# Program order for the GpSimd casts, spread weight loads and a wider skew in a fused retention and MLP-mixer kernel

## Chip, cores and metric

The kernel runs on one core of a Trainium2 chip. The metric is the device time of one execution in microseconds (us), as the median of several runs. Engines are called PE (TensorE matmul), PEld (its weight loads), DVE (VectorE), ACT (ScalarE), POOL (GpSimd) and SP (SyncE, which only issues transfers here).

## What is computed

Two layers, one behind the other, for 4 batches, 768 positions, 8 heads of 64 (512 channels):

```python
gamma = 1.0 - 2.0 ** (-5.0 - np.arange(H))
for t in range(S):                                   # retention, per head
    state = gamma * state + outer(k[t], v[t])
    y[t] = scale * q[t] @ state
x = y as [B, S, H * D]
xt = x.transpose(0, 2, 1)                            # token mixing
h = np.maximum(xt @ w_tok1, 0.0) @ w_tok2            # 768 -> 256 -> 768
u = x + h.transpose(0, 2, 1)
h2 = np.maximum(u @ w_ch1, 0.0) @ w_ch2              # channel mixing, 512 -> 1536 -> 512
return u + h2
```

Inputs, weights and output are float32 in DRAM; the matmuls take float16.

## The kernel before

**Tiling.** The sequence is cut into 6 chunks of 128 positions (`NC`), in two halves of 3 (`HC`). Heads go in pairs, 4 pairs per batch (`NP`, index `p`), so a pair fills 128 partitions. The retention is computed in its chunked form: within a chunk by a masked score matrix, across chunks by a running state `U`.

**Front.** `front(b, p)` (L137) does retention and token mixing of one batch and head pair and is a generator of 11 steps (`NS`), each ended by a `yield`:
- step 0: DVE scales k to float16 (L156, two instructions), POOL casts q (L158);
- step 1: PE transposes k (L167), ACT copies it out (L169), POOL casts v (L172);
- step 2: PE transposes q;
- step 3: PE forms k'v per chunk (L189 in batch 0, L192 later), DVE chains them into `U` (L197, L199), ACT and DVE write its float16 form (L201, L202);
- steps 4, 5: scores of either half (L211), masked by DVE into `am` (L214);
- steps 6, 7: output y of either half (L224, L226), scaled into `x` by ACT (L232) or, in the second half of batches 1 to 3, by DVE with the table `gyw` (L236), then cast to float16 by POOL (L237, one cast per half);
- step 8: first token matmul (L243, 12 matmuls over both halves of `x16`), ReLU on ACT (L245);
- step 9: second token matmul (L253), DVE adds it to `x` (L256), POOL casts the sum to `u16` (L257), once per half;
- step 10: PE transposes `u16` (L263), ACT copies it into `uT` (L265, L267).

**Back.** `back(b)` does channel mixing of a batch: for each half of the sequence 12 groups of 4 matmuls over `uT` and `wc1` (L288, ReLU in L291), then 3 output tiles of 12 matmuls over `wc2` (L296), a DVE add (L301) and a store from SP (L303). It needs `uT` of all four pairs.

**Order.** `fronts(b, skew)` interleaves the four generators of a batch: step `s` of pair `p` stands at `skew * p + s`, and steps at one place go by `s`. Front 0 runs alone with skew 4. After it, a list of planned times merges the steps of back `b` with those of front `b + 1`; the back's 47 planned us (`PERIOD`) hold 44 steps of the next front, which begin 10 planned us in for batch 1 and 9 before the back for later ones, and lie evenly on 28 planned us for batch 1. This is the order in which the program is written. A scheduler then simulates the machine with its own durations and may issue instructions of an engine in another order, by readiness and place; the order that it finds is fixed in each engine's queue, and every queue is worked off in order.

**Order edges.** `keep_in_program_order` (`pin`) ties an instruction behind the one that stands last before it on the same engine in the written program; it adds no wait. Before, the k, q and v casts (L156, L158, L172) are pinned; the casts L237 and L257 and the table's eight multiplications (L317) are not. `issue_after` ties the weight loads behind the v cast of pair 1 (`wt1`, `wt2`) and of pair 3 (all three `wc1`, all three `wc2`): L106 to L114, on POOL's queue, casting from float32 on the way.

**Loads.** `load(b, p)` (L126) issues k, q and v of a pair from SP, 128 x 768 float32 (0.39 MB) each. Those of batch 1 wait until the last of the three `wc1` loads has landed.

Of the kernel before, what the change touches and what calls it, by code (L numbers as in the profile page):

```python
# [13 lines left out]
ALU = mybir.AluOpType  # L14
# [3 lines left out]
def kernel(  # L18
# [11 lines left out]
    nc = tc.nc  # L30
    B, H, S, D = q.shape
    P = 128
# [22 lines left out]
    def bank():  # L55
        return ps.tile([P, 512], FP, name="acc")
# [16 lines left out]
    gy = const_p.tile([P, H], FP, name="gy")  # L73
# [6 lines left out]
    for p in range(NP):  # L80
# [5 lines left out]
        out=mask, in_=mask, compare_op=ALU.is_ge, fill=0.0,  # L86
        base=0, pattern=[[0, HC], [1, P]], channel_multiplier=-1,
    )
    gyw = const_p.tile([P, H, D], FP, name="gyw")
# [6 lines left out]
    wt1 = const_p.tile([P, NC, DT], F16, name="wt1")  # L96
    wt2 = const_p.tile([P, NJ, S], F16, name="wt2")
    NW = 3
    FW = NF // NW
    wc1 = [const_p.tile([P, NP, FW * P], F16, name=f"wc1_{i}") for i in range(NW)]  # L100
    wc2 = [const_p.tile([P, FW, C], F16, name=f"wc2_{i}") for i in range(NW)]

    def load_weights(stage):
        first = []
        if stage == 0:
            nc.gpsimd.dma_start(out=wt1, in_=moe_w_tok1.rearrange("(i p) j -> p i j", p=P))  # L106
            nc.gpsimd.dma_start(out=wt2, in_=moe_w_tok2.rearrange("(i p) j -> p i j", p=P))
        elif stage == 1:
            for i in range(NW):
                first.append(nc.gpsimd.dma_start(  # L110
                    out=wc1[i], in_=moe_w_ch1[:, i * FW * P:(i + 1) * FW * P].rearrange(
                        "(i p) j -> p i j", p=P)))
            for i in range(NW):
                nc.gpsimd.dma_start(  # L114
                    out=wc2[i], in_=moe_w_ch2[i * FW * P:(i + 1) * FW * P].rearrange(
                        "(i p) j -> p i j", p=P))
        return first


    loaded = {}  # L120
# [1 line left out]
    def load(b, p, after=None):  # L122
        got = []
        for nm, src in (("k", k), ("q", q), ("v", v)):
            t = load_p.tile([P, 2 * NC, D], FP, name=f"{nm}f")
            dma = nc.sync.dma_start(  # L126
                out=t, in_=src[b, 2 * p:2 * p + 2].rearrange("h (c p) d -> p (h c) d", p=P))
            if after is not None:
                tc.add_manual_dep(
                    dma.ins, after.ins.name,  # L130
                    mybir.DependencyInfo(mybir.DependencyClass.Sync, mybir.DependencyReason.DATA),
                    reason="the weights come first")
            got.append(t)
        loaded[b, p] = got
# [3 lines left out]
    def front(b, p):  # L138
# [3 lines left out]
        x, uT = xs[b]  # L142
        pc = slice(p * P, (p + 1) * P)
        kf, qf, vf = loaded.pop((b, p))
        first = b == 0
        pin = tc.keep_in_program_order

        def half(hf):
            return slice(hf * HC, (hf + 1) * HC)
# [4 lines left out]
        for j in range(2):  # L154
            h = 2 * p + j
# [61 lines left out]
        x16 = att_p.tile([P, NC, P], F16, name="x16", bufs=2)  # L217
        for hf in range(2):
            y = bank()
            for i in range(HC):  # L220
                c = hf * HC + i
                o = y[:, i * P:(i + 1) * P]
                if c > 0:
                    nc.tensor.matmul(o, qT[:, c * P:(c + 1) * P], R[:, c - 1], start=True, stop=False)  # L224
                for j in range(2):
                    nc.tensor.matmul(o[:, j * D:(j + 1) * D], ams[2 * hf + j][:, i], v16[:, c, j],  # L226
                                     start=(c == 0), stop=(c == 0 or j == 1))
            yv = y[:, :HC * P].rearrange("p (i d) -> p i d", d=P)
            if hf == 0 or first:
                for j in range(2):  # L230
                    h = 2 * p + j
                    nc.scalar.mul(x[:, half(hf), h * D:(h + 1) * D], yv[:, :, j * D:(j + 1) * D],  # L232
                                  gy[:, h:h + 1])
            else:
                g = gyw[:, 2 * p:2 * p + 2].rearrange("p (o h) d -> p o (h d)", o=1)
                nc.vector.tensor_tensor(x[:, half(hf), pc], yv, g.to_broadcast([P, HC, P]), ALU.mult)  # L236
            nc.gpsimd.tensor_copy(x16[:, half(hf)], x[:, half(hf), pc])  # L237
            yield
        h1 = att_p.tile([P, NJ, P], F16, name="h1", bufs=2)
        acc = bank()  # L240
# [6 lines left out]
        u16 = att_p.tile([P, NC, P], F16, name="u16", bufs=2)  # L247
        for hf in range(2):
            acc = bank()
            for i in range(HC):  # L250
                t = slice((hf * HC + i) * P, (hf * HC + i + 1) * P)
                for jt in range(NJ):
                    nc.tensor.matmul(acc[:, i * P:(i + 1) * P], wt2[:, jt, t], h1[:, jt],  # L253
                                     start=(jt == 0), stop=(jt == NJ - 1))
            xo = x[:, half(hf), pc]
            nc.vector.tensor_tensor(xo, xo, acc[:, :HC * P].rearrange("p (i d) -> p i d", d=P), ALU.add)  # L256
            nc.gpsimd.tensor_copy(u16[:, half(hf)], xo)  # L257
        yield
        tp = ps_tp.tile([P, 1024], F16, name="tp")
        for hf in range(2):  # L260
# [11 lines left out]
    def fronts(b, skew):  # L272
        gens = [front(b, p) for p in range(NP)]
        for _, s, p in sorted((skew * p + s, s, p) for p in range(NP) for s in range(NS)):
            yield s, p, next(gens[p])
# [3 lines left out]
    def back(b):  # L279

        x, uT = xs.pop(b)
        for sh in range(2):
            h2 = mlp_p.tile([P, NF, SH], F16, name="h2")
            for ft in range(NF):
                acc = bank()
                w = wc1[ft // FW]
                for ct in range(NP):
                    nc.tensor.matmul(acc[:, :SH], w[:, ct, (ft % FW) * P:(ft % FW + 1) * P],  # L288
                                     uT[:, ct, sh * SH:(sh + 1) * SH],
                                     start=(ct == 0), stop=(ct == NP - 1))  # L290
                nc.scalar.activation(h2[:, ft], acc[:, :SH], AF.Relu)  # L291
                yield
            for i in range(HC):
                acc = bank()
                for ft in range(NF):
                    nc.tensor.matmul(acc, h2[:, ft, i * P:(i + 1) * P], wc2[ft // FW][:, ft % FW],  # L296
                                     start=(ft == 0), stop=(ft == NF - 1))
                    if ft % 4 == 3 and ft < NF - 1:
                        yield
                o = o_p.tile([P, C], FP, name="o")  # L300
                nc.vector.tensor_tensor(o, x[:, sh * HC + i], acc, ALU.add)  # L301
                t0 = (sh * HC + i) * P
                nc.sync.dma_start(out=out[b, t0:t0 + P, :], in_=o)  # L303
                yield


    for p in range(NP):
        load(0, p)
    ch1 = None
    for s, p, ins in fronts(0, 4):  # L310
        if s == 1 and p in (1, 3):
            with tc.issue_after(ins.ins):
                ch1 = load_weights(p // 3)
    for p in range(NP):
        load(1, p, after=ch1[-1])
    for h in range(H):
        nc.gpsimd.tensor_scalar(gyw[:, h], gyw[:, h], gy[:, h:h + 1], None, ALU.mult)  # L317


    FRONT_US, BACK_US, LEAD = 16.0, 31.0, 9.0  # L320
# [3 lines left out]
    def add(steps, times, kind):  # L324
        for n, t in enumerate(times):
            todo.append((t, len(todo), steps, kind))

    for b in range(B):
        t0 = b * PERIOD
        gen = back(b)  # L330
        us = BACK_STEPS
        span = PERIOD if b + 1 < B else BACK_US
        run = 0.0
        times = []
        for d in us:
            times.append(t0 + run / BACK_US * span)
            run += d
        add(gen, times, ("back", b))
        if b + 1 < B:
            f0 = t0 + 10.0 if b == 0 else t0 - LEAD  # L340
            f1 = t0 + PERIOD - LEAD
            n = NP * NS
            add(fronts(b + 1, 5), [f0 + (f1 - f0) * i / n for i in range(n)], ("front", b + 1))
    for t, _, gen, (kind, b) in sorted(todo, key=lambda e: e[:2]):
        got = next(gen)
        if kind == "front" and b + 1 < B and got[0] == 3:
# [31 lines left out]
```

## Time and profile before

| | us |
|---|---|
| median of 3 runs (247.86 to 248.69) | 248.13 |
| the profiled execution | 248.53 |
| its span, first to last instruction | 246.8 |
| PE busy | 204.7 |
| DVE busy | 120.4 |
| ACT busy | 105.8 |
| POOL busy | 69.3 |

The profiled execution lies 0.40 us above the median, and 1.7 us of it lie outside the span. All positions below are us from the span's start. In a timeline the columns are start, duration, engine, line, operation, output <- inputs, shapes and count, and in brackets the idle time of that engine just before, with what ended it.

### The profile page before, as it was taken

To read this page: it belongs to the slowest core of one execution; us is meant where nothing else is said; L and a number is where in the kernel's file an instruction comes from. 1 tells how busy PE (TensorE), PEld (TensorE's weight loads), DVE (VectorE), ACT (ScalarE), POOL (GpSimd) and SP (SyncE) were. 2 spreads that over 40 slices of the span, in tenths; PEclk is the share of its full clock that TensorE was granted. 3 is DMA by queue.
4 is the path that set the end of the run, shared out by engine and by line. 5 is a ranking of instruction groups with operands and counts; after the bars stand their busy time and mean duration, and the time that the engine had idled before them with its cause. 6 is when DMAs were issued, how large, how long until landed. Compare 5 with 4: busy or idle time off the path is not lost.

```text
span 246.8 us, 4741 instructions
## 1 busy us (share of the span) xinstructions
PE 204.7 (83%) x1908; PEld 129.2 (52%) x1908; DVE 120.4 (49%) x287; ACT 105.8 (43%) x219; POOL 69.3 (28%) x120
## 2 busy tenths in 40 slices
PE   0466865004999999899999999799999999999994
PEld 0355644003666577565766566457665764554641
DVE  5276764000319896649647772586468723103012
ACT  2142451201574368533872566148724661450710
POOL 2862574004401424252150522601414121000000
PEclk9999997755899999999999999999999999999999
DMA  8999419999999999129895570111011101202112
GB/s 162 217 216 223 78 13 200 204 219 218 219 216 225 234 187 213 34 64 214 194 170 111 129 150 0 45 42 45 0 46 44 45 0 42 88 0 85 45 42 85
DMA packets 82198, 29.41 MB, mean 119 GB/s; under 512 B 75008, under 2 KB 79104, under 8 KB 82176
## 3 DMA queue, kind: packets, MB, share of 16 engines
q1 hardware_dynamic: 77952, 25.17, 50.2%
q0 software_dynamic: 4224, 3.93, 9.9%
q8 instruction: 15, 0.25, 0.4%
q14 instruction: 7, 0.06, 0.1%
HBM read 26.74 MB, written 6.29 MB: 134 GB/s over the span
## 4 chain that ended last, share of the span: by engine, by line
PE 61%; issue 15%; DVE 7%; POOL 6%; DMA 5%; SPq 2%; ACT 2%; DVEq 0%; POOLq 0%; ACTq 0%
PE acc L288 21%; PE acc L296 19%; PE acc L243 5%; PE acc L253 4%; PE tp L167 3%; DMA vf<-in_v_dram 3%; SPq L126 2%; DMA wt<-in_moe_w_tok_dram 2%; PE acc L211 2%; PE tp L263 2%; DVE k L156 2%; POOL u L257 2%; DVE x L256 2%; PE acc L226 2%; POOL x L237 1%
## 5 line engine op out<-in xcount | busy, mean ns | idle before, releaser
L288 PE MATMUL acc<-uT,wc 128*128 128x384 f16 x384 | 73.3, 329 | 0.0
L296 PE MATMUL acc<-wc,h 128*128 128x512 f16 x288 | 71.0, 379 | 0.0
L291 ACT ACTIVATE h<-acc 128x384 f16<-128x384 f32 x96 | 46.9, 496 | 31.4 <-PE acc L288 31.3
L288 PEld LDWEIGHTS <-wc 128*128 128x128 f16 x384 | 34.5, 98 | 18.9 <-issue 0.5
L296 PEld LDWEIGHTS <-h 128*128 128x128 f16 x288 | 25.5, 98 | 23.2
L214 DVE TENSOR_TENSOR am<-acc,mask 128x384 f16<-128x384 f32 x64 | 33.9, 551 | 5.2 <-PE acc L211 4.8
L301 DVE TENSOR_TENSOR o<-x,acc 128x512 f32<-128x512 f32 x24 | 16.4, 685 | 38.7 <-PE acc L296 38.7
L237 POOL CAST x<-x 128x384 f16<-128x384 f32 x32 | 16.3, 512 | 61.8 <-issue 45.1
L257 POOL CAST u<-x 128x384 f16<-128x384 f32 x32 | 16.5, 533 | 54.2 <-DVE x L256 54.0
L256 DVE TENSOR_TENSOR x<-x,acc 128x384 f32<-128x384 f32 x32 | 16.5, 549 | 28.9 <-PE acc L253 28.4
L263 PE MATMUL tp<-ident,u 128*128 128x128 f16 x96 | 10.3, 229 | 17.7 <-POOL u L257 16.4
L199 DVE SCALAR_TENSOR_TENSOR U<-U,gp,acc 128x128 f32<-128x128 f32 (+1 forms) x64 | 21.1, 329 | 2.3
L243 PE MATMUL acc<-x,wt 128*128 128x128 f16 x192 | 15.9, 230 | 6.0 <-POOL x L237 3.6
L169 ACT COPY kT<-tp 128x768 f16<-128x768 f16 x16 | 12.8, 802 | 15.0 <-PE tp L167 13.5
L158 POOL CAST q<-qf 128x768 f16<-128x768 f32 x16 | 14.0, 872 | 17.3 <-DMA qf<-in_q_dram 17.3
L263 PEld LDWEIGHTS <-u 128*128 128x128 f16 x96 | 6.5, 101 | 23.2 <-POOL u L257 21.0
L243 PEld LDWEIGHTS <-wt 128*128 128x128 f16 x192 | 13.3, 103 | 9.8 <-issue 4.5
L232 ACT ACTIVATE x<-acc,gy 128x192 f32<-128x192 f32 x40 | 14.8, 428 | 8.1 <-PE acc L226 8.1
L267 ACT COPY uT<-tp 128x768 f16<-128x768 f16 x12 | 9.6, 797 | 19.7 <-PE tp L263 19.7
L236 DVE TENSOR_TENSOR x<-acc,gyw 128x384 f32<-128x384 f32 x12 | 6.7, 558 | 22.4 <-PE acc L226 22.4
L156 DVE TENSOR_SCALAR k<-kf,gk 128x384 f16<-128x384 f32 x32 | 17.2, 574 | 0.8 <-DMA kf<-in_k_dram 0.6
L226 PE MATMUL acc<-v,am 128*128 128x64 f16 x192 | 16.6, 201 | 0.9 <-DVE am L214 0.8
(47 smaller groups left out, 198.3 us busy)
## 6 DMA issues: line engine op xcount, KB each, us to landing
kf<-in_k_dram SPq DMA_DIRECT2D x16, 384.0 KB, 5.7
qf<-in_q_dram SPq DMA_DIRECT2D x16, 384.0 KB, 6.2
vf<-in_v_dram SPq DMA_DIRECT2D x16, 384.0 KB, 6.3
out_dram<-o SPq DMA_DIRECT2D x24, 256.0 KB, 2.0
wc<-in_moe_w_ch_dram POOLq DMA_DIRECT2D x6, 512.0 KB, 10.2
wt<-in_moe_w_tok_dram POOLq DMA_DIRECT2D x2, 384.0 KB, 6.7
```

Source lines behind the costliest of these rows:

```text
L156: pin(nc.vector.tensor_scalar(k16[:, :, j, :], kf[:, j * NC:(j + 1) * NC, :], gk[:, h:h + 1], None, ALU.mult))
L199: nc.vector.scalar_tensor_tensor(U[:, c], U[:, c - 1], gp[:, p:p + 1], o, ALU.mult, ALU.add)
L214: nc.vector.tensor_tensor(am, a[j][:, :HC], mask, ALU.mult)
L226: nc.tensor.matmul(o[:, j * D:(j + 1) * D], ams[2 * hf + j][:, i], v16[:, c, j], start=(c == 0), stop=(c == 0 or j == 1))
L237: nc.gpsimd.tensor_copy(x16[:, half(hf)], x[:, half(hf), pc])
L243: nc.tensor.matmul(acc[:, jt * P:(jt + 1) * P], wt1[:, i, jt * P:(jt + 1) * P], x16[:, i], start=(i == 0), stop=(i == NC - 1))
L256: nc.vector.tensor_tensor(xo, xo, acc[:, :HC * P].rearrange("p (i d) -> p i d", d=P), ALU.add)
L257: nc.gpsimd.tensor_copy(u16[:, half(hf)], xo)
L263: nc.tensor.transpose(tp[:, c * P:(c + 1) * P], u16[:, c], ident16)
L288: nc.tensor.matmul(acc[:, :SH], w[:, ct, (ft % FW) * P:(ft % FW + 1) * P], uT[:, ct, sh * SH:(sh + 1) * SH], start=(ct == 0), stop=(ct == ...
L291: nc.scalar.activation(h2[:, ft], acc[:, :SH], AF.Relu)
L296: nc.tensor.matmul(acc, h2[:, ft, i * P:(i + 1) * P], wc2[ft // FW][:, ft % FW], start=(ft == 0), stop=(ft == NF - 1))
```

## The change

1. The casts L237 and L257 and the eight table multiplications L317 are pinned too, so that all of POOL's work from the first cast on goes in written order. The q cast of batch 1 is then behind all casts of batch 0.
2. The weight loads become a generator whose loads are pinned one by one: `wt1` and `wt2` behind the v cast of pair 1 as before; `wc1[0]` behind the v cast of pair 3; then one load behind each of the steps 6, 7 and 9 that follow in front 0, until all six are out. The loads of batch 1 still wait for the third `wc1` (`dmas[4]`).
3. Front 1 is interleaved with skew 8 in place of 5; its planned stretch stays.

```diff
+    pin = tc.keep_in_program_order
+    def weights():
+        yield pin(nc.gpsimd.dma_start(out=wt1, ...))
+        yield pin(nc.gpsimd.dma_start(out=wt2, ...))
+        for i in range(NW):
+            yield pin(nc.gpsimd.dma_start(out=wc1[i], ...))
+        for i in range(NW):
+            yield pin(nc.gpsimd.dma_start(out=wc2[i], ...))
...
-            nc.gpsimd.tensor_copy(x16[:, half(hf)], x[:, half(hf), pc])
+            pin(nc.gpsimd.tensor_copy(x16[:, half(hf)], x[:, half(hf), pc]))
...
-            nc.gpsimd.tensor_copy(u16[:, half(hf)], xo)
+            pin(nc.gpsimd.tensor_copy(u16[:, half(hf)], xo))
...
-    ch1 = None
-    for s, p, ins in fronts(0, 4):
-        if s == 1 and p in (1, 3):
-            with tc.issue_after(ins.ins):
-                ch1 = load_weights(p // 3)
+    w = weights()
+    dmas = []
+    for s, p, _ in fronts(0, 4):
+        if (s, p) == (1, 1):
+            dmas += [next(w), next(w)]
+        elif (s, p) == (1, 3) or (len(dmas) > 2 and s in (6, 7, 9)):
+            dmas += [ins for ins in [next(w, None)] if ins is not None]
+    dmas += list(w)
     for p in range(NP):
-        load(1, p, after=ch1[-1])
+        load(1, p, after=dmas[4])
     for h in range(H):
-        nc.gpsimd.tensor_scalar(gyw[:, h], gyw[:, h], gy[:, h:h + 1], None, ALU.mult)
+        pin(nc.gpsimd.tensor_scalar(gyw[:, h], gyw[:, h], gy[:, h:h + 1], None, ALU.mult))
...
-            add(fronts(b + 1, 5), [f0 + (f1 - f0) * i / n for i in range(n)], ("front", b + 1))
+            add(fronts(b + 1, 8 if b == 0 else 5), [f0 + (f1 - f0) * i / n for i in range(n)], ("front", b + 1))
```

## Rows read from the trace of the kernel before

**Rows 1.** The page: busy by engine, and GB/s in 40 slices of 6.17 us.
```profile
PE 204.7 (83%) x1908; PEld 129.2 (52%) x1908; DVE 120.4 (49%) x287; ACT 105.8 (43%) x219; POOL 69.3 (28%) x120
...
GB/s 162 217 216 223 78 13 200 204 219 218 219 216 225 234 187 213 34 64 214 194 170 111 129 150 0 45 42 45 0 46 44 45 0 42 88 0 85 45 42 85
```

**Rows 2.** Windows: stretch, its us, busy by engine, PE clock, DMA share, GB/s.
```profile
43.00:58.00 15.00, 0.71 (x10) 0.58 (x9) 0.00 (x0) 1.55 (x5) 0.97 (x2) 0.61 1.27 213
...
66.00:80.00 14.00, 13.80 (x129) 8.57 (x126) 6.63 (x18) 8.79 (x18) 0.96 (x2) 1.00 1.17 221
...
106.00:156.00 50.00, 49.47 (x491) 30.89 (x488) 31.03 (x68) 25.92 (x53) 15.54 (x26) 1.00 0.60 127
```

**Rows 3.** PE's longest wait: line, releaser, us in total, times, longest.
```profile
PE tp L263 <- POOL u L257: 16.4, 3, 14.7
```

**Rows 4.** Timeline of POOL, 8 to 60 us.
```profile
8.95 3.36 POOL L317 TENSOR_SCALAR gyw<-gyw,gy 128x64 f32<-128x64 f32 x8
...
29.08 0.83 POOL L158 CAST q<-qf 128x768 f16<-128x768 f32 x1
...
32.78 0.96 POOL L257 CAST u<-x 128x384 f16<-128x384 f32 x2
...
34.46 2.28 POOL L110 DMA_DIRECT2D wc<-in_moe_w_ch_dram x3
...
38.92 0.56 POOL L237 CAST x<-x 128x384 f16<-128x384 f32 x1
42.33 0.51 POOL L257 CAST u<-x 128x384 f16<-128x384 f32 x1 [2.86 <-DVE x L256]
57.03 0.83 POOL L158 CAST q<-qf 128x768 f16<-128x768 f32 x1 [14.19 <-DMA qf<-in_q_dram]
...
58.26 0.96 POOL L237 CAST x<-x 128x384 f16<-128x384 f32 x2
59.16 0.83 POOL L172 CAST v<-vf 128x768 f16<-128x768 f32 x1
```

**Rows 5.** Timeline of PE, 40 to 117 us.
```profile
40.81 1.44 PE L253 MATMUL acc<-h,wt 128*128 128x128 f16 x12 [0.53 <-ACT h L245]
...
60.92 1.44 PE L253 MATMUL acc<-h,wt 128*128 128x128 f16 x12 [0.53 <-ACT h L245]
...
72.74 0.44 PE L192 MATMUL acc<-v,k 128*128 128x128 f16 x5
...
96.44 0.44 PE L192 MATMUL acc<-v,k 128*128 128x128 f16 x5
...
108.60 0.34 PE L263 MATMUL tp<-ident,u 128*128 128x128 f16 x3
...
116.08 0.81 PE L288 MATMUL acc<-uT,wc 128*128 128x384 f16 x4
```

**Rows 6.** Timeline of DVE, the sums of batch 0, pair 1.
```profile
31.56 1.01 DVE L256 TENSOR_TENSOR x<-x,acc 128x384 f32<-128x384 f32 x2
```

**Rows 7.** Timeline of ACT, y of pair 2 (second half), pair 3 (first).
```profile
35.40 0.73 ACT L232 ACTIVATE x<-acc,gy 128x192 f32<-128x192 f32 x2 [0.30 <-PE acc L226]
...
42.82 0.73 ACT L232 ACTIVATE x<-acc,gy 128x192 f32<-128x192 f32 x2 [2.06 <-PE acc L226]
```

**Rows 8.** Line L110, the three wc1 loads: durations, then landing times.
```profile
L110 POOL DMA_DIRECT2D wc<-in_moe_w_ch_dram x3: 750/762/792, 34.5 to 36.0; - x3
...
DMA to landing us min/median/max: 5.6/7.4/9.2
```

**Rows 9.** Timeline of SP, the first load of batch 1.
```profile
45.28 0.37 SPq L126 DMA_DIRECT2D kf<-in_k_dram  x1
```

**Rows 10.** Timeline of POOL, 123 to 126 us, in the steady state.
```profile
123.86 1.10 POOL L257 CAST u<-x 128x384 f16<-128x384 f32 x2 [4.47 <-DVE x L256]
124.91 0.95 POOL L158 CAST q<-qf 128x768 f16<-128x768 f32 x1
```

**Rows 11.** Tile kf: durations of the k casts on DVE, min/median/max ns.
```profile
L156 DVE TENSOR_SCALAR k<-kf,gk x32: 414/420/1057, 4.6 to 187.5; 128x384 f16<-128x384 f32 x32
```

More of the change, by code (lines that the diff above doesn't have):

```diff
@@ L101 @@
     wc2 = [const_p.tile([P, FW, C], F16, name=f"wc2_{i}") for i in range(NW)]
[L103 to L117, printed above, removed]
+    pin = tc.keep_in_program_order
+    def weights():
+        yield pin(nc.gpsimd.dma_start(out=wt1, in_=moe_w_tok1.rearrange("(i p) j -> p i j", p=P)))
+        yield pin(nc.gpsimd.dma_start(out=wt2, in_=moe_w_tok2.rearrange("(i p) j -> p i j", p=P)))
+        for i in range(NW):
+            yield pin(nc.gpsimd.dma_start(
+                out=wc1[i], in_=moe_w_ch1[:, i * FW * P:(i + 1) * FW * P].rearrange(
+                    "(i p) j -> p i j", p=P)))
+        for i in range(NW):
+            yield pin(nc.gpsimd.dma_start(
+                out=wc2[i], in_=moe_w_ch2[i * FW * P:(i + 1) * FW * P].rearrange(
+                    "(i p) j -> p i j", p=P)))
     loaded = {}
@@ L145, in front @@
         first = b == 0
-        pin = tc.keep_in_program_order
         def half(hf):
```

## The prediction

> **What bounds the kernel now.** I read the busy shares first, then the windows, then PE's waits, and only then POOL's timeline. PE is the busiest engine with 204.7 of 246.8 us [rows 1], but not evenly. From 66 us on it is full: 13.80 of 14 us, later 49.47 of 50 [rows 2]. In 43 to 58 us it worked 0.71 of 15 us, DVE nothing, while transfers ran at 213 GB/s [rows 2]. So there are two regimes: up to about 60 us the kernel waits, behind that it is PE's work, and whatever brings the start of back 0 forward shortens the run by as much, as long as PE has something to do. The wait list names the hole: PE's transposes L263 waited 14.7 us at one go for the cast L257 on POOL [rows 3]. POOL's timeline says why: it cast the first half of `u` of pair 2 at 42.33, then its next instruction was the q cast of batch 1, which stood until 57.03 for its load; only then came the second half of `u`, and at 58.26 the two x casts of pair 3, with no idle time before them [rows 4]. The scheduler had put a cast whose data was not there ahead of three that were ready: x of pair 3 was scaled by 43.55 in its first half [rows 7]. A smaller hole of the same kind lies ahead of it: the second x cast of pair 2 ran at 38.92, behind six weight loads issued without a break from 34.46 [rows 4], though its input was done at 35.40 + 0.73 = 36.13 [rows 7].
>
> **Part 1, front 0 on POOL.** With every POOL instruction in written order I lay out the queue behind the q cast of pair 3, which ends at 29.91 [rows 4]; ahead of that I take no difference.
> - v of pair 3, which stood just ahead of 34.46, follows at once and takes 0.83 like the other v casts [rows 4], to 30.74. Its load is there: the rate fell to 78 GB/s in 24.7 to 30.9 us and to 13 behind that [rows 1], so batch 0's loads had ended. `wc1[0]` takes 0.76 [rows 8], so it goes out at 30.75, 3.71 ahead of 34.46.
> - u of pair 1: its sums end at about 32.05 and 32.57 [rows 6], so two casts of 0.51 end at 33.1; `wc1[1]` to 33.8, x (first half) of pair 2 to 34.35, `wc1[2]` to 35.1.
> - x (second half) of pair 2: u of pair 1 starts at 32.05, 0.73 ahead of its old 32.78 [rows 4], and what hung on it comes as much earlier, so the input is ready at 36.13 - 0.73 = 35.4. The cast moves from 38.92 to 35.4, by 3.5 us.
> - With it go L253 of pair 2 (40.81 to 37.3) [rows 5] and u: 42.33 to 38.83 [rows 4]. Two u casts end at 39.85, `wc2[1]` at 40.6, x first half at 41.1 (its input is there: 43.55 - 3.5 = 40.05), `wc2[2]` at 41.85, x second half at 42.35. The two issues between them are on the path, 1.5 us.
> - From the end of that cast to L253 pair 2 took 40.81 - 39.48 = 1.33 us, so pair 3's L253 starts at 43.7. It started at 60.92 [rows 5]: **17.2 us earlier**. I count nothing for the clock, which was granted 0.61 on 43 to 58 us [rows 2], behind the wait: L253 is priced at the 1.44 that it had there.
>
> The table's 3.36 us [rows 4] leave the start and stand behind the last u cast, at some 46 to 49.5 us. There POOL would wait for the first load of batch 1 anyway; the cover is gone if that load landed by 46, and then they cost at most 3.36. At their old place nothing is gained, as the next casts there waited for their own loads.
>
> **Part 2, the weights and batch 1's loads.** Three `wc1` loads landed 5.6, 7.4 and 9.2 us after their issue [rows 8], with issues 0.76 apart, so one takes about 2.6 us of transfer. The last landed at 45.2 and released the loads of batch 1 at 45.28 [rows 9]. Now the first goes out 3.71 earlier, and the third (34.35) well before its turn of transfer, so batch 1's loads start at about 41.6. Ahead of or beside the first three stand the three `wc2`, 3 x 2.6 = 7.8 us, and the loads' own 3 x 0.39 MB at 213 GB/s [rows 2] = 5.55: v of pair 0 should land 13.35 us behind, at 54.9 (old start plus the same: 58.6, which fits between q's cast at 57.03 and v's at 59.16 [rows 4]). All `wc2` are in by then. With 55.2 for v and 0.83 for its cast, L192 of batch 1 can run at 56.05. PE would come to it at 72.74 [rows 5] - 17.2 = 55.5: **a new wait of 0.5 us**. So the gain is 72.74 - 56.05 = **16.7 us**, set by batch 1's first v. Its bounds: v landing as early as q did (57.03 - 3.7), then no wait and 17.2; batch 1's loads starting no earlier than now, then 59.16 + 0.83 - 55.5 = 4.5 of wait and 12.7. I take the layout's value since the three issues that decide it are early in the queue.
>
> On the issue cost, the trace has 0.75 to 0.79 us for each `wc1` [rows 8], and k casts on DVE that take 0.42 in the middle and 1.06 at the longest [rows 11], so something does hold DVE up at times. The Trainium skill, "SBUF — State Buffer", section "SBUF: two separate sides", warns of what it calls the "DVE blocks DMA" trap: a POOL-issued load can't have its descriptors written while DVE runs in certain fast modes. By its example (620 ns alone, 3100 ns overlapped, in the section on the bandwidth-pool intuition) the five issues ahead of casts on the path would cost an estimated 12.4 us more, and the sum would be some 244; the three issues of rows 8, none above 0.79, speak against that.
>
> **Part 3, skew 8.** The same 44 steps lie on the same 28 planned us, 0.64 each, some 0.68 real (50 us per 47 planned). Step 3 of pair 1 moves from place 11 to place 14, 2.0 us later: 11 steps or 7.5 us behind pair 0's, at 63.5, where v of pair 1 (54.9 + 5.55 + 0.83 = 61.3) is there. With skew 5 it would come at 61.5, just about with its load. Step 3 of pair 3 moves from 33 to 36, so front 1 ends some 2.0 us later; before, its last transposes (108.60) stood 7.5 us ahead of back 1's first matmuls (116.08) [rows 5], so this is covered by the rest of back 0. Cost between 0 and 2.0; I take 0.5, near the covered end.
>
> **Part 4, pins in batches 1 to 3.** In the steady state POOL already goes in written order, u of a pair, then q of the next but one [rows 10]; batches 2 and 3 follow that pattern. Nothing; if a pin held x behind a late load, 1.66 (a q and a v cast) per pair.
>
> **Sum.** 16.7 - 0.5 = 16.2 us off the profiled 248.53 is 232.3; that execution stands 0.4 above the median, so **231.9**. On its own this case spans 229.5 (17.2, and two L253 at the upper of the clock's two levels, half of 1.44 each) to 235.4 (12.7).
>
> **Rivals.**
> - *Loads bind:* the hole moves into front 1. If batch 1's loads start at 45.28 as now, or SP issues them later, PE waits 4.5 us at pair 0 and the skew's 2.0 come on top: 248.1 - 17.2 + 6.5 = 237.4. For it: transfers are saturated in 43 to 58 us and compute moves 17 us forward, loads only 3.7. Against: the new place of `wc1`.
> - *Issues and DVE collide:* each of five issues waits for one DVE instruction, 0.5 us (half of rows 6's 1.01): 2.5 more, 234.4. This is the mechanism that the page on SBUF names above.
> - *No effect:* the q cast was not the true cause, or another queue holds batch 0 as long: 248.1. Against it stands that the three casts behind q ran without any idle time.
> - *Slower:* the wider skew leaves a pair of front 1 alone for 5 of its steps. From L192 to its last transposes pair 3 took 108.60 - 96.44 = 12.2 us [rows 5], of which PE works some 4 itself (a quarter of the planner's 16 us for a front); if the matmuls of back 0 don't stand between, PE waits up to 8 us a pair, 32 in all: 264. It turns into a loss where more than 16.2 of these 32 us are uncovered. Against: PE was 13.80 of 14 us busy through front 1's start [rows 2], and the scheduler may fill such gaps with the back's matmuls.
>
> **Chances.** Forecast 0.75, loads bind 0.14, collision 0.03, no effect 0.03, slower 0.05. A measurement of this kernel tells about 0.3%, 0.7 us. Faster 0.92, same 0.03, slower 0.05. The range takes the forecast's own ends and the loads' rival: 229.0 to 237.5.
>
> **What would show it.** Right: POOL's timeline has all of batch 0's casts ahead of the q cast of batch 1; PE's 14.7 us wait is gone; L253 of pair 3 near 43.7; SP's first load of batch 1 near 41.6; L192 near 56 with at most a short wait for v; PE full behind that. Wrong: a wait of several us of L167 or L192 for a POOL cast of batch 1 (loads bind), weight loads on POOL well above 0.8 us (collision), or PE idle between 60 and 100 us for DVE or ACT (skew).

## The result and the profile after

The changed kernel takes **240.7 us** (239.23 to 243.74, 4 runs) against 248.0 us before (247.63 to 248.69, 4 runs): ratio 0.968, 95% interval 0.962 to 0.975. It is faster by 7.3 us where 16.2 were forecast, and lies outside the range of 229.0 to 237.5. The profiled execution (243.74 us, mean PE clock 0.979) is a slow one that the ratio leaves out; the fastest, 239.23, had a clock of 1.000.

Up to 57 us the changed kernel does nearly what was laid out. POOL's timeline of the changed kernel, end of front 0 (answers to [rows 4]):

```profile
38.06 0.97 POOL L255 CAST u<-x 128x384 f16<-128x384 f32 x2 [1.80 <-DVE x L254]
38.98 0.74 POOL L114 DMA_DIRECT2D wc<-in_moe_w_ch_dram  x1
39.72 0.52 POOL L235 CAST x<-x 128x384 f16<-128x384 f32 x1
40.16 0.74 POOL L114 DMA_DIRECT2D wc<-in_moe_w_ch_dram  x1
40.90 0.52 POOL L235 CAST x<-x 128x384 f16<-128x384 f32 x1
43.88 0.97 POOL L255 CAST u<-x 128x384 f16<-128x384 f32 x2 [2.47 <-DVE x L254]
44.84 3.36 POOL L318 TENSOR_SCALAR gyw<-gyw,gy 128x64 f32<-128x64 f32 x8
54.45 0.82 POOL L156 CAST q<-qf 128x768 f16<-128x768 f32 x1 [6.25 <-DMA qf<-in_q_dram]
```

All of batch 0's casts now stand ahead of the q cast of batch 1, which waits for its load with nothing behind it that is ready. PE's 14.7 us wait [rows 3] is gone. PE's timeline of the changed kernel, 42 to 62 us (answers to [rows 5]; line numbers are one or two lower than before):

```profile
42.66 0.83 PE L251 MATMUL acc<-h,wt 128*128 128x128 f16 x12 [0.53 <-ACT h L243]
...
45.52 5.85 PE L286 MATMUL acc<-uT,wc 128*128 128x384 f16 x35
53.54 0.51 PE L165 MATMUL tp<-ident,k 128*128 128x128 f16 x6 [2.17 <-DVE k L154]
53.88 1.08 PE L286 MATMUL acc<-uT,wc 128*128 128x384 f16 x4
55.33 0.82 PE L165 MATMUL tp<-ident,q 128*128 128x128 f16 x6 [0.37 <-POOL q L156]
55.95 1.90 PE L294 MATMUL acc<-wc,h 128*128 128x512 f16 x4
57.66 0.48 PE L190 MATMUL acc<-v,k 128*128 128x128 f16 x5
...
58.34 1.04 PE L294 MATMUL acc<-wc,h 128*128 128x512 f16 x4
...
59.58 0.82 PE L294 MATMUL acc<-wc,h 128*128 128x512 f16 x3
60.24 0.22 PE L224 MATMUL acc<-v,am 128*128 128x64 f16 x2
60.30 0.38 PE L294 MATMUL acc<-wc,h 128*128 128x512 f16 x1
61.87 0.23 PE L222 MATMUL acc<-r,qT 128*128 128x128 f16 x1 [1.19 <-DVE r L200]
```

L251 of pair 3 starts at 42.66 (forecast 43.7, before 60.92). L190 of batch 1, the mark on which the forecast's gain was read, runs at 57.66 (forecast 56.05, before 72.74): 15.1 us ahead. But the span ends only 4.8 us earlier (242.0 against 246.8), so **10.3 us are lost behind that mark**. PE's waits of the changed kernel, 46 to 105 us, and the windows of the same stretch (columns as in [rows 2]):

```profile
PE acc L222 <- DVE r L200: 3.3, 3, 1.2
PE acc L241 <- POOL x L235: 2.4, 3, 1.1
PE tp L165 <- DVE k L154: 2.2, 1, 2.2
PE tp L165 <- POOL q L156: 0.4, 1, 0.4
PE acc L251 <- ACT h L243: 0.3, 1, 0.3
```

```profile
52.00:70.00 18.00, 13.76 (x114) 8.36 (x115) 7.84 (x18) 4.98 (x9) 5.39 (x8) 0.81 1.20 218
70.00:80.00 10.00, 7.64 (x71) 4.58 (x70) 6.54 (x15) 2.85 (x7) 2.75 (x4) 0.91 1.16 243
80.00:100.00 20.00, 18.66 (x190) 12.23 (x188) 11.85 (x28) 12.19 (x25) 5.13 (x9) 0.96 0.89 161
```

Behind the mark PE waits 6.0 us for pieces of front 1's own chain (r, x and h: 3.3 + 2.4 + 0.3), where the kernel before waited 0.8 us in all in its own front 1 (64 to 110 us). The other 4.3 us are what is left over, not a measured term; the clock can account for them, as it was granted 0.81 on 52 to 70 us of this execution, and the fastest run, at 1.000, is 4.5 us shorter: four L294 took 1.90 us at 55.95 and 1.04 at 58.34, one at the lower and one at the upper level.

### The profile page after: what moved, and what is told of

The parts are those of the page before. It is cut to its first block, busy times and chain, and to the rows that moved or that the text cites. A ratio compares the mean times of both kernels' runs of the same rounds, so it can differ in the third digit from the quotient of the medians.

```text
span 242.0 us, 4739 instructions
## 1 busy us (share of the span) xinstructions
PE 207.9 (86%) x1908; PEld 129.8 (54%) x1908; DVE 121.1 (50%) x287; ACT 106.4 (44%) x219; POOL 69.3 (29%) x120
## 4 chain that ended last, share of the span: by engine, by line
PE 63%; DMA 11%; issue 9%; DVE 6%; POOL 5%; SPq 3%; ACT 1%; DVEq 0%; POOLq 0%; ACTq 0%
PE acc L286 21%; PE acc L294 20%; PE acc L241 5%; PE tp L165 5%; DMA qf<-in_q_dram 5%; PE acc L251 5%; DMA vf<-in_v_dram 3%; SPq L125 3%; DMA wt<-in_moe_w_tok_dram 3%; DVE k L154 2%; PE acc L209 2%; POOL x L235 2%; PE tp L261 2%; DMA out_dram<-o 2%; PE acc L224 1%
## 5 line engine op out<-in xcount | busy, mean ns | idle before, releaser
L294 PE MATMUL acc<-wc,h 128*128 128x512 f16 x288 | 72.6, 386 | 0.0
L294 PEld LDWEIGHTS <-h 128*128 128x128 f16 x288 | 26.1, 99 | 23.9 <-issue 0.8
L212 DVE TENSOR_TENSOR am<-acc,mask 128x384 f16<-128x384 f32 x64 | 34.0, 550 | 4.6 <-PE acc L209 4.3
L299 DVE TENSOR_TENSOR o<-x,acc 128x512 f32<-128x512 f32 x24 | 16.5, 685 | 39.0 <-PE acc L294 39.0
L255 POOL CAST u<-x 128x384 f16<-128x384 f32 x32 | 16.0, 521 | 48.5 <-DVE x L254 48.4
L154 DVE TENSOR_SCALAR k<-kf,gk 128x384 f16<-128x384 f32 x32 | 18.2, 610 | 9.3 <-DMA kf<-in_k_dram 9.2
L241 PE MATMUL acc<-x,wt 128*128 128x128 f16 x192 | 16.2, 230 | 6.9 <-POOL x L235 4.4
L241 PEld LDWEIGHTS <-wt 128*128 128x128 f16 x192 | 13.4, 103 | 10.8 <-issue 6.2
L230 ACT ACTIVATE x<-acc,gy 128x192 f32<-128x192 f32 x40 | 14.7, 426 | 9.1 <-PE acc L224 9.1
L251 PE MATMUL acc<-h,wt 128*128 128x128 f16 x192 | 15.2, 234 | 1.9 <-ACT h L243 1.9
L222 PE MATMUL acc<-r,qT 128*128 128x128 f16 x80 | 13.1, 228 | 4.2 <-DVE r L200 4.2
L224 PEld LDWEIGHTS <-am 128*128 128x128 f16 x192 | 13.9, 102 | 4.6 <-DVE am L212 1.6
```

Source lines behind the costliest of these rows:

```text
L154: pin(nc.vector.tensor_scalar(k16[:, :, j, :], kf[:, j * NC:(j + 1) * NC, :], gk[:, h:h + 1], None, ALU.mult))
L212: nc.vector.tensor_tensor(am, a[j][:, :HC], mask, ALU.mult)
L241: nc.tensor.matmul(acc[:, jt * P:(jt + 1) * P], wt1[:, i, jt * P:(jt + 1) * P], x16[:, i], start=(i == 0), stop=(i == NC - 1))
```

## The experiments

Theory O (order): the written order at skew 8 leaves too few matmuls of back 0 between the links of a pair's chain. Theory L (loads): batch 1's loads come late, and the skew is not to blame. Each run is compared with runs of the kernel before on the same chip.

**Skew 5 in the changed kernel.**

```diff
-            add(fronts(b + 1, 8 if b == 0 else 5), ...)
+            add(fronts(b + 1, 5), ...)
```

> The changed kernel with skew 5 in front 1, as before the change; pins and spread weight loads stay. Theory O (order): the time lost after the first L190/L192 of batch 1 comes from the written order at skew 8, which puts both y halves of a pair and its token matmul behind too few matmuls of back 0. Then the waits for r and x in front 1 (3.3 and 2.4 us) go and the time is 232 to 235. Theory L (loads): PE runs into batch 1's loads, whatever the skew. Then pair 1 waits for its v in place of r and x, and the time stays at 238 to 242.

232.69 us (232.44 to 232.98), ratio 0.937 (0.934 to 0.940). Theory O. PE's waits in 46 to 105 us, then two windows:

```profile
PE tp L165 <- DVE k L154: 1.7, 1, 1.7
PE acc L190 <- POOL v L170: 0.7, 2, 0.4
PE tp L165 <- POOL q L156: 0.7, 1, 0.7
PE tp L261 <- POOL u L255: 0.5, 1, 0.5
PE acc L241 <- POOL x L235: 0.3, 1, 0.3
```

```profile
52.00:70.00 18.00, 15.26 (x156) 8.82 (x157) 12.92 (x31) 6.36 (x13) 6.70 (x10) 1.00 1.15 220
70.00:80.00 10.00, 9.87 (x116) 6.92 (x114) 7.05 (x16) 7.50 (x17) 4.23 (x7) 1.00 1.06 228
```

The waits for r are gone, of those for x 0.3 is left, and the clock stays at 1.00 in these windows. Besides 0.5 for u, what remains are waits for the loads of batch 1, 3.1 us. The fastest run of the changed kernel, 239.23 us at a clock of 1.000, is still 6.2 us above the slowest here, about the 6.0 us of waits; so the larger part of the loss does not hang on the clock.

**Skew 8 alone, on the kernel before.**

```diff
-            add(fronts(b + 1, 5), ...)
+            add(fronts(b + 1, 8 if b == 0 else 5), ...)
```

> The kernel before with skew 8 in front 1 as its only change; POOL's hole in front 0 stays, so batch 1's loads are there long before PE wants them. Theory O: PE's queue in front 1 has the changed kernel's order, so it waits some 6 us more than before and the clock may fall: 253 to 257. Theory L: nothing waits for loads here, so 247 to 249.

256.35 us (255.58 to 257.67), ratio 1.033 (1.028 to 1.037). The hole in front 0 is still there, the loads of batch 1 are early, and the wider skew still costs 7.7 us. PE's timeline:

```profile
73.18 0.44 PE L192 MATMUL acc<-v,k 128*128 128x128 f16 x5
...
73.83 1.04 PE L296 MATMUL acc<-wc,h 128*128 128x512 f16 x4
...
75.07 0.82 PE L296 MATMUL acc<-wc,h 128*128 128x512 f16 x3
...
75.78 0.38 PE L296 MATMUL acc<-wc,h 128*128 128x512 f16 x1
77.36 0.23 PE L224 MATMUL acc<-r,qT 128*128 128x128 f16 x1 [1.19 <-DVE r L202]
```

The same 4 + 3 + 1 matmuls stand between L192 and the first use of r as in the changed kernel, and the wait is the same 1.19 us. This takes theory L away as the cause of the 6 us.

**Pins alone, on the kernel before.** Pins on L237, L257 and L317; weight loads and skew as before.

```diff
-            nc.gpsimd.tensor_copy(x16[:, half(hf)], x[:, half(hf), pc])
+            pin(nc.gpsimd.tensor_copy(x16[:, half(hf)], x[:, half(hf), pc]))
...
-            nc.gpsimd.tensor_copy(u16[:, half(hf)], xo)
+            pin(nc.gpsimd.tensor_copy(u16[:, half(hf)], xo))
```

> The kernel before with the pins on L237, L257 and L317 as its only change; all six wc loads stand in one block behind the v cast of pair 3, skew 5. The block delays the casts of u of pair 1 and what follows by up to 3 us against the spread loads, but releases batch 1's loads some 2 us earlier. Theory O: 233 to 237. Theory L: 238 to 242, as the loads set the pace.

232.3 us (231.9 to 232.59), ratio 0.935 (0.932 to 0.938): the same as with spread loads, and 0.7 below the range given for theory O. PE's timeline:

```profile
43.97 1.43 PE L253 MATMUL acc<-h,wt 128*128 128x128 f16 x12 [0.53 <-ACT h L245]
...
48.09 5.85 PE L288 MATMUL acc<-uT,wc 128*128 128x384 f16 x35
...
56.50 0.44 PE L192 MATMUL acc<-v,k 128*128 128x128 f16 x5 [0.38 <-POOL v L172]
```

The long run of back 0 starts 2.3 us later than with spread loads (48.09 against 45.77 in the skew-5 run), yet L192 comes at 56.50 against 56.84: both meet the loads of batch 1, released at 42.03 and 42.02, and not 2 us apart as was expected.

**Loads of batch 1 released earlier, skew 8.**

```diff
-        load(1, p, after=dmas[4])
+        load(1, p, after=dmas[3])
```

> The changed kernel with batch 1's loads released by the second wc1 load in place of the third, some 2.6 us earlier. Theory O: only the 2.5 us that PE waits for k and q of pair 0 can go, the waits for r and x stay: 238 to 240.5. Theory L: PE's idle time in front 1 follows the loads: 237 or less.

242.48 us (241.47 to 243.35), ratio 0.977 (0.972 to 0.982): no gain, and 2.0 above the top of the range given for theory O. The first load goes out at 39.42 in place of 42.63, and over the whole run PE's waits for r and x stay (columns as in [rows 3]):

```profile
PE acc L222 <- DVE r L200: 4.2, 4, 1.2
PE acc L241 <- POOL x L235: 4.2, 6, 1.1
```

In 46 to 105 us they are the same 3.3 and 2.4 us as in the changed kernel's profile, although this execution kept a clock of 1.00 on 52 to 70 us. So the waits do not come from the lower clock that the changed kernel's profile shows there.

**Skew 6**, in the same line of the changed kernel as the first run.

> The changed kernel with skew 6 in front 1. Theory O: what costs is the number of back-0 matmuls that stand in PE's queue between a pair's L190 and its first L222. For pair 0 that is 8 at skew 8, 16 at skew 5 and 12 here, 0.216 us each, against a DVE chain of about 4 us. So the wait for r falls from 1.2 to about 0.3 us a pair: 233 to 235.5. If skew itself costs in proportion to its width, a third of the 8 us: 235.5 or more.

234.89 us (233.9 to 236.34), ratio 0.943 (0.939 to 0.948). One wait for r is left, 1.1 us, and 0.6 for x. PE's timeline:

```profile
61.82 0.23 PE L222 MATMUL acc<-r,qT 128*128 128x128 f16 x1 [1.14 <-DVE r L200]
```

This is pair 0. The 12 matmuls that were expected for it did not come: between its L190 (57.40) and this line stand 8, two groups of four L294, as many as at skew 8, and the wait is nearly the same. Pair 1 has 13 L294 there, besides work of pair 0, and does not wait. The time lies inside the range given for theory O and only 0.6 below what a proportion to the width would give, so this run alone would not decide.

**Skew 8 with two empty steps ahead of y.**

```diff
+        if b == 1:
+            yield
+            yield
         x16 = att_p.tile([P, NC, P], F16, name="x16", bufs=2)
```

(The number of steps of batch 1 rises from 11 to 13 where it is counted.)

> The changed kernel, skew 8, with two empty steps between the scores and y of each pair of batch 1, so that 12 back-0 matmuls stand between L190 and the first L222 of pair 0, and pairs still hardly overlap. Theory O: the waits for r nearly go although the skew stays 8: 233.5 to 236.5. If a pair that runs alone is slow for another reason (ACT, POOL, bank turns): 239 or more.

233.84 us (233.17 to 235.53), ratio 0.940 (0.935 to 0.944). The skew is still 8 and most of its cost is gone. PE's timeline:

```profile
56.48 0.44 PE L190 MATMUL acc<-v,k 128*128 128x128 f16 x5 [1.22 <-POOL v L170]
56.76 1.03 PE L297 MATMUL acc<-wc,h 128*128 128x512 f16 x4
...
58.16 0.39 PE L297 MATMUL acc<-wc,h 128*128 128x512 f16 x1
...
58.75 1.68 PE L297 MATMUL acc<-wc,h 128*128 128x512 f16 x7
60.27 0.22 PE L227 MATMUL acc<-v,am 128*128 128x64 f16 x2
60.33 0.22 PE L225 MATMUL acc<-r,qT 128*128 128x128 f16 x1
```

Twelve matmuls stand there now, and r is met without a wait at 3.85 us behind L190. By itself this run does not settle that the width is harmless: 52 steps lie on the 28 planned us of the former 44, so the pairs move closer too. From L190 of pair 0 to that of pair 1 it is 8.2 us here, 12.9 in the changed kernel and 8.9 at skew 6. The comparison with skew 6 says more: at nearly the same distance between pairs, pair 0 waits 1.14 us with 8 matmuls in between and not at all with 12.

The count on PE is not all of it. DVE's queue is fixed as well: the write of r (L200) starts 3.1 us behind L190 here, with two masks (L212) ahead of it, and 3.8 us in the changed kernel, with four. Pair 1 of the changed kernel has twelve L294 between L190 (70.59) and its first L222 and waits all the same, since DVE's queue puts two output adds of back 0 (L299, at 70.80 and 74.49) around the links of its chain:

```profile
75.61 0.23 PE L222 MATMUL acc<-r,qT 128*128 128x128 f16 x1 [1.17 <-DVE r L200]
```

So what costs is how close a pair's dependent steps stand in the order of both queues; how much of it DVE's order makes was not tested by itself.

**Weight loads still earlier, skew 5.** The six `wc` loads behind steps (9,0), (6,1), (7,1), (1,3), (9,1), (6,2), written as (step, pair).

> Skew 5, all pins, and the six wc loads issued one by one but each some steps earlier, from behind the u casts of pair 0 on, in the stretch where transfers idle. If the start of batch 1's loads is what hides the gain of the spread loads, they now start near 38 us, front 1's first L190 runs some 2 us earlier, and the time is 229.5 to 231.5. If front 0 itself sets it, each issue in its casts delays it by 0.75 and the time is 232.5 to 235.

231.33 us (229.96 to 232.41), ratio 0.930 (0.926 to 0.934). PE's timeline:

```profile
30.07 0.51 PE L165 MATMUL tp<-ident,k 128*128 128x128 f16 x6 [2.50 <-DVE k L154]
...
53.97 0.44 PE L190 MATMUL acc<-v,k 128*128 128x128 f16 x5
```

L190 comes 2.9 us ahead of the skew-5 run's 56.84, without a wait. But PE now waits 2.5 us in front 0 for k of pair 3, and nine first token matmuls of pair 1 (L241), which stand behind those transposes in PE's queue here, wait with them. The load of k is not what they wait for: DVE cast k at 28.69, right behind other work, with no idle time before it.

**Loads of batch 1 released earlier, skew 5**, the same edit as above.

> Skew 5, all pins, spread weight loads, and batch 1's loads released by the second wc1 load in place of the third. The same bytes stand ahead of batch 1's first v, so L190 moves by less than 1 us: 231.5 to 233. If the release alone held the loads back, L190 moves by 2.6 us: 229.5 to 230.5.

232.65 us (232.44 to 232.99), ratio 0.934 (0.931 to 0.936); L190 at 56.91. The first load goes out at 39.32 in place of 42.02 and L190 does not move, so the release is not the limit. That the bytes ahead of batch 1's first v are is borne out by the runs with earlier weights.

**Only the table pinned, on the kernel before.**

```diff
-        nc.gpsimd.tensor_scalar(gyw[:, h], gyw[:, h], gy[:, h:h + 1], None, ALU.mult)
+        tc.keep_in_program_order(
+            nc.gpsimd.tensor_scalar(gyw[:, h], gyw[:, h], gy[:, h:h + 1], None, ALU.mult))
```

> The kernel before with one edit: only the eight table multiplications L317 are pinned. They then stand behind the last u cast of batch 0, and the q cast of batch 1, which is pinned behind them, can no longer pass batch 0's casts. If the hole in front 0 came from that one edge, the 14 us wait goes with it; the weight loads keep their old place, so batch 1's loads still start at 45.3, its first v lands near 58.9, L192 of batch 1 runs near 59.8 and the time is 235 to 236.5. If the pins on L237 and L257 are what counts, 240 or more.

236.96 us (236.07 to 237.03), ratio 0.955 (0.952 to 0.957), 0.5 above the expected range. POOL's and PE's timelines:

```profile
48.12 0.98 POOL L257 CAST u<-x 128x384 f16<-128x384 f32 x2 [2.47 <-DVE x L256]
...
58.08 0.82 POOL L158 CAST q<-qf 128x768 f16<-128x768 f32 x1 [5.64 <-DMA qf<-in_q_dram]
```

```profile
60.71 0.44 PE L192 MATMUL acc<-v,k 128*128 128x128 f16 x5 [0.38 <-POOL v L172]
```

One edge takes the whole hole away: the q cast of batch 1 had been pinned behind table multiplications that were themselves free to float to 8.95 us [rows 4], so its pin held nothing. What the pins on the casts add (232.3 against 237.0, on different chips) is an earlier v cast of pair 3 (29.63 against 33.84) and so earlier weights and loads: batch 1's loads start at 45.46 here and at 42.03 there.

**The best of these, side by side.** In the first of the three, the six loads stand behind (6,1), (7,1), (1,3), (9,1), (6,2), (7,2).

> Skew 5, all pins, and the six wc loads one by one, two places earlier than in the change, so that the first goes out near 27 us, as batch 0's last loads land. Batch 1's loads start near 38.5, L190 of batch 1 runs near 54, and k of pair 3 is not delayed as in the version with still earlier weights: 229.5 to 231. If weight loads and batch 0's loads still collide: 231 to 233.

> The version with the earliest weights once more, beside its rivals on one chip: 230 to 232.

> The changed kernel with skew 5 once more, beside its rivals on one chip: 232 to 233.5. If it is not over 1 us behind the versions with earlier weights, batch 1's loads were not what hid the gain of the spread loads.

On one chip (before 247.83): **229.8 us** for the middle placement (229.47 to 231.09, ratio 0.928, 0.925 to 0.930), 231.43 for the earliest (0.934, 0.932 to 0.937), 233.07 for the change's own placement at skew 5 (0.940, 0.937 to 0.942). PE's timeline of the middle one:

```profile
42.29 0.83 PE L251 MATMUL acc<-h,wt 128*128 128x128 f16 x12 [0.53 <-ACT h L243]
...
53.36 0.44 PE L190 MATMUL acc<-v,k 128*128 128x128 f16 x5 [0.18 <-POOL v L170]
```

Batch 1's loads start at 38.73, and PE meets its first v with 0.18 us of wait. In the profile of the earliest version PE waits 3.05 us for k of pair 3 in front 0, ahead of the same matmuls of pair 1, and the long run of back 0 starts at 47.47 us, 2.3 later than the 45.15 here. This version beats the kernel before by 18.0 us, and lies 10.9 below the changed one's median, which was not measured beside it.

## Why the prediction was wrong

**Part 1 held.** The hole came from the q cast ahead of ready casts. L253/L251 of pair 3 was forecast at 43.7 and ran at 42.66; of the surplus 0.5 us was there before (L251 of pair 2 ran at 36.84, 37.3 forecast), and the rest fits the clock, which stayed at the upper level there (0.83 us for L251 in place of the 1.44 that was priced).

**Part 2 held in kind, and was short.** Batch 1's loads started at 42.63 (41.6 forecast) and, as forecast, set the pace: L190 ran at 57.66 (56.05). But the working looked at v alone, a wait of 0.5 us (and took 55.2 us for it where its own sum gives 54.9), and in the changed kernel's profile L190 shows no wait for v; at skew 5 it is 0.39 us. PE's queue already stood at the transposes of k (2.17 us) and q (0.37), and eight matmuls of back 0 queued behind those waits ran late too, four of them at the lower clock (1.90 us). The spread of the weight loads brought nothing by itself, as pins alone show: front 0 was faster by some 2 us, and the loads took them back.

**Part 3 is the step that failed.** "Cost between 0 and 2.0; I take 0.5, near the covered end." It measured 7.7 us alone (256.35 against 248.67) and some 8 in the changed kernel (240.7 against 232.69, each near 248 before); 6.0 us of it stand in the profile as PE's waits for r, x and h. The working asked when front 1 ends and whether loads come in time, that is, about the distance between pairs. What it left out is the distance within a pair: at skew 8 a pair's y stands three planned steps behind its L190 (places 3 and 6), at skew 5 five (3 and 8). With that the scheduler placed, for pair 0, 8 matmuls of 0.216 us in between in place of 16, against a chain on DVE of 4.2 us from L190 to the first use of r (57.66 to 61.87). The wait for x is of the same kind: between y of pair 0 and its first L241 PE has nothing else in its queue at skew 8 and waits 1.11 us (63.72); at skew 5 matmuls of pair 1 (L190) and four L294 stand there, and it does not wait. Each queue is fixed, so PE stood still although back 0 had work.

**The rivals.** "Slower" had this mechanism, its place and its price, and 0.05; its chain was uncovered by 6.0 of the 32 us, plus the clock, so it took about half of the gain and not all of it. Its counter-argument, that PE was full through front 1's start, was read at skew 5 and could not hold for 8. "Loads bind" is not what took the time. "Issues and DVE collide" fell: the `wc` issues took 0.74 to 0.90 us beside DVE's work. Without part 3's edit the same working gives 248.1 - 16.7 = 231.4; the skew-5 run measured 232.69.

## What to carry to other kernels

- Where an order is written by hand and then fixed in queues, count the filler between two links of a dependent chain and set it against the chain's time in the trace, with what else stands in the queues of the engines that work on the chain; widening the distance between streams narrows the distance within each. Price a new order from its own places, not from how full the engine was under the old one.
- An instruction pinned behind one that is free to float is free itself; look at what a pin's other end does. And when a hole is closed, ask which transfer is reached next and what bytes stand ahead of it: moving those into a stretch where transfers idle was worth 3.3 us here, moving them one place further ahead gave half of that back (231.43 us), as PE's fixed order then had transposes that waited 2.5 to 3.1 us ahead of matmuls on the path of front 0.

## What was not expected of the hardware

- The granted clock fell inside front 1 in some executions: 0.81 on 52 to 70 us of the changed kernel's profile, with PE busy 13.76 of 18 us. But the run with loads released earlier at skew 8 kept 1.00 on the same stretch with PE busy for the same 13.76 us, and had 0.83 on 70 to 80 us. The skew-5 version kept 1.00 in both, with 15.26 of 18 us busy, and its runs stay within 232.44 to 232.98 us, where the changed kernel varies from 239.23 to 243.74. Why one execution falls and another doesn't stays open.
- The first load of batch 1 was issued at 42.63 and its k cast began at 52.73, 10.1 us later, behind and beside three `wc2` loads; the median k load of that run, of the same 0.39 MB, took 5.4 us from issue to landing.
